# Nine dV tiles stored in three parts each, around three groups of DMA engines, in place of four tiles around one engine

## The chip, the cores and the metric

The kernel runs on one core of one Trainium2 chip. The metric is the device time of the slowest (here the only) core, in microseconds. Before the change the median of three runs was 402.31 us (402.08 to 402.5). The profiled span is some 2 us shorter than the device time of the same run (400.8 against 402.56 us), so spans are compared with spans and times with times.

## The reference

One decode step through a mix of attention and a small dense layer, and the gradients of everything. Only the attention's caches matter for the time: each is 32 heads of 4096 x 128 in bf16, 1 MB a head, read once; and their gradients have the same size and are written once.

```python
q = (x @ wq).reshape(B, Sq, H, Dh).transpose(0, 2, 1, 3)        # H = 32, Sq = 1, Dh = 128
scores = jnp.einsum("bhqd,bhkd->bhqk", q, k_cache) * (Dh ** -0.5)
p = softmax(scores, axis=-1)
o = jnp.einsum("bhqk,bhkd->bhqd", p, v_cache)
a = o.transpose(0, 2, 1, 3).reshape(B, Sq, H * Dh) @ wo
b = dense_mish(B_x, w1, b1, w2)                                 # cut
out = g * a + (1 - g) * b                                       # g = sigmoid(sum(x * gate_w))
# returned: out and the gradients of x, k_cache, v_cache, wq, wo, w1, b1, w2, gate_w
```

## The kernel before

One head after another is loaded, multiplied and stored. The loads and a few last stores are issued by SyncE (queue q1 of the profile), the gradients of K and V by GpSimd (queue q0). A tile has 128 rows (partitions) of 8 KB; a store of all 128 rows puts 8 rows on each of the 16 DMA engines.

```python
outs = ctx.enter_context(tc.tile_pool(name="outs", bufs=5))          # dK and dV tiles share it
...
def load_wo(g):
    if g < NG:
        wos[g] = wts.tile([P, G, D], BF16, name="wo_g", tag="wo_g", bufs=3)
        nc.sync.dma_start(wos[g][:], wo_v[g])                        # L136; dwo is stored from the same tile
...
def dv_half(h, half):
    st = sts[h]
    if half == 0:
        st["dV"] = outs.tile([P, J, Dh], BF16, name="dV_sb", tag="dVK")
    outer(st["dV"], st["p"], ..., half)                              # cut
    if half == 1:
        if h % 7 == 5 and h < H - 3:                                 # heads 5, 12, 19, 26
            spread(h // 7, dVv[h], st["dV"])
        else:
            ring(h).dma_start(dVv[h], st["dV"][:])

def spread(i, dst, t):
    src = t[:].rearrange("p j d -> p (j d)")
    out = dst.rearrange("p j d -> p (j d)")
    if i % 3 == 0:
        nc.gpsimd.inc_swdge_sem([], [], mode="reset_dge_cursor")
    for a, b in (((120, 125), (0, 120), (125, 128)), ((0, 14), (14, 119), (119, 128)), ((0, 8), (8, 128)))[i % 3]:
        nc.gpsimd.dma_start(out[a:b, :], src[a:b, :], max_dma_last_dim=J * Dh)
```

`spread` cuts a store into parts whose row counts decide which DMA engines take how many rows. With the cursor reset, a part of 5 rows goes to the first five engines, one row each; the part of 120 rows to the fifteen that follow, so that the fifth engine counted from the reset, "position 4", gets none; the part of 3 to positions 4, 5 and 6. Position 4 ends with 2 rows of the tile instead of 8.

## Time and profile before

| | before |
|---|---|
| time, median (range), 6 runs | 402.40 us (402.08 to 402.96) |
| span of the profiled run | 400.8 us |
| bytes over the DMA engines | 164.92 MB |
| mean rate from 12 to 375 us | 420 GB/s |
| engine time idle after 387.5 us | 3.8 us of all 16 (worked out in the prediction) |

### The profile page before, as it was taken

How to read it: one execution, taken by the hardware profiler on the slowest of the kernel's cores; microseconds unless marked ns; L12 is line 12 of the kernel's file. 1: busy time of each engine (PE TensorE's matmuls, PEld its weight loads, DVE VectorE, ACT ScalarE, POOL GpSimd, SP SyncE). 2: the span in 40 equal slices, each digit the busy share in tenths (PEclk: the TensorE clock that was granted, in tenths of full speed). 3: DMA queues.
4: the chain of work that ended last, by engine and by line, in shares of the span. 5: the costliest groups of instructions: out<-in, count | busy, mean ns of one | idle time of the engine just before them, and what ended most of it. 6: DMA issues, size and time to landing. Idle time of an engine off the chain costs nothing.

```text
span 400.8 us, 13361 instructions
## 1 busy us (share of the span) xinstructions
PE 301.0 (75%) x5752; PEld 266.0 (66%) x5752; DVE 303.1 (76%) x783; ACT 178.2 (44%) x403; POOL 47.0 (12%) x94
## 2 busy tenths in 40 slices
PE   0788888678888788768879788838888888888300
PEld 0577888567777677658868778718777678877200
DVE  3339666556799999767658999836999997898860
ACT  1455454325545555326533555604545545555000
POOL 0001111021110111211110112101111121111000
PEclk9899999959999999969977999967999999999755
DMA  8999999999999999999999999999999999999995
GB/s 292 417 407 405 418 426 421 407 423 421 424 421 424 422 422 416 422 424 424 419 424 426 422 422 417 417 425 424 421 421 424 424 423 418 425 420 418 424 383 229
DMA packets 28359, 164.92 MB, mean 412 GB/s; under 512 B 3260, under 2 KB 3964, under 8 KB 12556
## 3 DMA queue, kind: packets, MB, share of 16 engines
q1 hardware_dynamic: 17136, 93.41, 56.5%
q0 software_dynamic: 11104, 70.64, 42.3%
q8 instruction: 45, 0.74, 0.7%
q14 instruction: 14, 0.11, 0.1%
q10 hardware_dynamic: 60, 0.01, 0.0%
HBM read 82.03 MB, written 82.03 MB: 409 GB/s over the span
## 4 chain that ended last, share of the span: by engine, by line
DVE 38%; DMA 32%; PE 20%; ACT 5%; issue 3%; ACTq 0%; SPq 0%
DMA Kn<-in_A_k_cache_dram 30%; DVE dK_sb L605 9%; DVE dV_sb L605 9%; PE tr L580 8%; DVE junk L378 5%; ACT tT L582 4%; DVE junk L278 3%; PE sA L660 3%; PE sA L589 3%; PE sB L713 3%; DVE junk L530 2%; DVE wo_g L367 1%; DMA vec_rows<-in_gate_w_dram 1%; DVE dj L700 1%; DVE dwq_t L732 1%
## 5 line engine op out<-in xcount | busy, mean ns | idle before, releaser
L582 ACT COPY tT<-tr 128x512 f32<-128x512 f32 x256 | 142.4, 587 | 127.8 <-PE tr L580 126.0
L589 PEld LDWEIGHTS <-tT 128*128 128x128 bf16 x2048 | 79.8, 98 | 40.3 <-ACT tT L582 34.6
L580 PE MATMUL tr<-ident_f,Kn 128*128 128x128 f32 x512 | 81.6, 297 | 9.2 <-DMA Kn<-in_A_k_cache_dram 9.2
L605 DVE TENSOR_TENSOR dV_sb<-p_bf,qd 128x2048 bf16<-128x2048 bf16 x64 | 78.0, 1218 | 0.2 <-issue 0.2
L605 DVE TENSOR_TENSOR dK_sb<-ds_bf,qd 128x2048 bf16<-128x2048 bf16 x64 | 77.7, 1216 | 0.0
L580 PE MATMUL tr<-ident_f,Vn 128*128 128x128 f32 x512 | 72.9, 278 | 0.0
L580 PEld LDWEIGHTS tr<-ident_f,Kn 128*128 128x128 f32 x512 | 61.0, 152 | 10.4 <-issue 10.4
L589 PE MATMUL sA<-qd,tT 128*128 128x48 bf16 x1024 | 48.7, 187 | 23.8 <-ACT dq_all L718 12.7
L580 PEld LDWEIGHTS tr<-ident_f,Vn 128*128 128x128 f32 x512 | 56.3, 142 | 0.0
L589 PE MATMUL sB<-qd,tT 128*128 128x48 bf16 x1024 | 46.0, 183 | 0.0
L660 PEld LDWEIGHTS <-Vn 128*128 128x128 bf16 x1024 | 30.2, 95 | 10.9 <-issue 10.9
L660 PE MATMUL sA<-e_bf,Vn 128*128 128x48 bf16 x1024 | 30.7, 183 | 8.1 <-DVE zs L680 6.5
L622 POOL DMA_DIRECT2D out_dram<-dK_sb x30 | 17.2, 574 | 138.9 <-DVE rz L682 86.5
L713 PE MATMUL sB<-ds_bf,Kn 128*128 128x48 bf16 x1024 | 32.2, 186 | 1.4 <-DVE ds_bf L702 1.4
L664 DVE TENSOR_REDUCE m<-sA 128x1 f32<-128x32 f32 x32 | 6.1, 189 | 32.9 <-PE sA L589 26.4
L713 PEld LDWEIGHTS <-Kn 128*128 128x128 bf16 x1024 | 29.5, 98 | 1.6 <-issue 1.6
L635 POOL DMA_DIRECT2D out_dram<-dV_sb x26 | 14.1, 542 | 135.8 <-DVE o_all L705 53.4
L278 DVE SCALAR_TENSOR_TENSOR junk<-wo_g,da_bc 128x640 bf16<-128x640 bf16 x32 | 26.2, 820 | 1.7 <-ACT da_bc L229 1.1
L378 DVE SCALAR_TENSOR_TENSOR junk<-wq_g,dq_bc 128x1024 bf16<-128x1024 bf16 (+1 forms) x25 | 25.1, 1005 | 0.2
L700 DVE TENSOR_SCALAR_CACHE_REDUCE dj<-sB,rz 128x128 f32<-128x128 f32 x32 | 11.1, 346 | 13.2 <-PE sB L694 13.2
L289 PE MATMUL q_ps<-wq_g,cols_bf 128*128 128x512 bf16 x40 | 13.1, 469 | 10.5 <-DMA wq_g<-in_A_wq_dram 10.5
L684 ACT ACTIVATE p_bf<-e_bf,rz 128x64 bf16<-128x64 bf16 x32 | 11.1, 348 | 13.9 <-DVE rz L682 11.1
(148 smaller groups left out, 268.8 us busy)
## 6 DMA issues: line engine op xcount, KB each, us to landing
Kn<-in_A_k_cache_dram SPq DMA_DIRECT2D x32, 1024.0 KB, 24.0
Vn<-in_A_v_cache_dram SPq DMA_DIRECT2D x32, 1024.0 KB, 28.0
out_dram<-dK_sb POOLq DMA_DIRECT2D x30, 1024.0 KB, 11.8
out_dram<-dV_sb POOLq DMA_DIRECT2D x26, 1024.0 KB, 11.8
wq_g<-in_A_wq_dram SPq DMA_DIRECT2D x4, 1280.0 KB, 23.2
wo_g<-in_A_wo_dram SPq DMA_DIRECT2D x8, 640.0 KB, 17.6
out_dram<-wo_g POOLq DMA_DIRECT2D x7, 640.0 KB, 11.8
out_dram<-dwq_t SPq DMA_DIRECT2D x4, 896.0 KB, 17.5
```

The lines of the kernel that those rows point to most:

```text
L278: nc.vector.scalar_tensor_tensor(junk[:, 0:D], in0=wos[g][:, i, :], scalar=1.0, in1=da_bc[:], op0=ALU.mult, op1=ALU.mult, accum_out=gp["do ...
L289: nc.tensor.matmul(q_ps[:], lhsT=x_bf[:, rc:rc + 1].to_broadcast([P, P]), rhs=wq[:, rc, off:off + GD], start=(rc == 0), stop=(rc == RC - 1))
L378: nc.vector.scalar_tensor_tensor(junk[:, c0:c1], in0=wqs[w][:, rc, c0:c1], scalar=1.0, in1=dq_bc[:, w * WG * Dh + c0:w * WG * Dh + c1], op ...
L580: nc.tensor.transpose(tp[:, t, :], flat[:, k * P:(k + 1) * P], ident_f[:])
L582: nc.scalar.copy(sb[:].rearrange("p a b -> p (a b)"), tp[:].rearrange("p a b -> p (a b)"))
L589: nc.tensor.matmul(out[:, 2 * k:2 * k + W], lhsT=tb[:, t, par, :], rhs=vec[:, par, :].unsqueeze(1).to_broadcast([P, W // 2, 2]), start=(pa ...
L605: nc.vector.tensor_tensor(dst[:, a:b, :].rearrange("p j (a b) -> p j a b", b=2), col[:, a:b, :].unsqueeze(2).to_broadcast([P, n, Dh // 2, 2]),
L622: ring(h).dma_start(dKv[h], st["dK"][:])
L635: ring(h).dma_start(dVv[h], st["dV"][:])
L660: nc.tensor.matmul(O, lhsT=vts[h][:, j, :], rhs=st["e"][:, j:j + 1].to_broadcast([P, W]), start=(j == 0), stop=(j == J - 1))
L700: nc.vector.tensor_scalar(dj[:], PT, rz[:], None, ALU.mult, ALU.add, accum_out=dd[:])
L713: nc.tensor.matmul(DQ, lhsT=kts[h][:, j, :], rhs=ds[:, j, 0:1].to_broadcast([P, W]), start=(j == 0), stop=(j == J - 1))
```

## The change

Its intent: five engines run dry some microseconds before the others, so rows are to be moved away from all that end late, not from position 4 alone. Nine tiles are cut in parts: two leave out positions 9 to 14, three leave out 0 to 3, four leave out 4. "Leave out" is again 2 rows for 8. This is the whole diff:

```diff
         if half == 1:
-            if h % 7 == 5 and h < H - 3:
-                spread(h // 7, dVv[h], st["dV"])
+            if h in SPREAD:
+                spread(SPREAD[h], dVv[h], st["dV"])
             else:
                 ring(h).dma_start(dVv[h], st["dV"][:])
 
-    def spread(i, dst, t):
+    N4 = ((120, 125), (0, 120), (125, 128))
+    N6 = ((113, 128), (0, 100), (100, 113))
+    N03 = ((124, 128), (0, 108), (108, 124))
+    SPREAD = {3: N03, 6: N6, 9: N4, 12: N03, 15: N6, 18: N4, 21: N03, 24: N4, 27: N4}
+
+    def spread(parts, dst, t):
         src = t[:].rearrange("p j d -> p (j d)")
         out = dst.rearrange("p j d -> p (j d)")
-        if i % 3 == 0:
-            nc.gpsimd.inc_swdge_sem([], [], mode="reset_dge_cursor")
-        for a, b in (((120, 125), (0, 120), (125, 128)), ((0, 14), (14, 119), (119, 128)), ((0, 8), (8, 128)))[i % 3]:
+        nc.gpsimd.inc_swdge_sem([], [], mode="reset_dge_cursor")
+        for a, b in parts:
             nc.gpsimd.dma_start(out[a:b, :], src[a:b, :], max_dma_last_dim=J * Dh)
```

## The prediction

> **What bounds the kernel now.** I read the shares by engine first, then the slices of the DMA row, the queues, the chain that ended last, the windows, and last the DMA queue's own waits and issues.
>
> ```profile
> span 400.8 us, 13361 instructions
> ...
> PE 301.0 (75%) x5752; PEld 266.0 (66%) x5752; DVE 303.1 (76%) x783; ACT 178.2 (44%) x403; POOL 47.0 (12%) x94
> ...
> DMA  8999999999999999999999999999999999999995
> ...
> DMA packets 28359, 164.92 MB, mean 412 GB/s; under 512 B 3260, under 2 KB 3964, under 8 KB 12556
> ...
> q8 instruction: 45, 0.74, 0.7%
> ```
>
> No compute engine is above 76%, while the DMA row shows 9 in every slice but the first and last: 164.92 MB cross 16 DMA engines that never rest. The compute part of the chain of waits (DVE 38%, DMA 32%) only tells that DVE is next in line. The last line, instruction fetch, looks negligible; it is not, since it falls on some engines alone.
>
> ```profile
> 12.00:375.00 363.00, 296.83 (x5713) 263.39 (x5712) 287.99 (x727) 175.33 (x397) 46.05 (x82) 0.94 1.01 420
> 375.00:387.50 12.50, 1.33 (x25) 0.90 (x24) 11.03 (x38) 0.15 (x1) 0.00 (x0) 0.51 1.01 423
> 387.50:390.50 3.00, 0.28 (x1) 0.09 (x1) 0.05 (x1) 0.25 (x1) 0.00 (x0) 0.50 0.70 291
> 390.50:394.50 4.00, 0.00 (x0) 0.00 (x0) 0.00 (x0) 0.00 (x0) 0.00 (x0) 0.50 0.95 377
> 394.50:397.00 2.50, 0.00 (x0) 0.00 (x0) 0.00 (x0) 0.00 (x0) 0.00 (x0) 0.50 0.64 250
> 397.00:399.50 2.50, 0.00 (x0) 0.00 (x0) 0.00 (x0) 0.00 (x0) 0.00 (x0) 0.50 0.28 101
> ```
>
> The last two columns are the DMA share and GB/s. Up to 387.5 us all 16 engines work (1.01 counts a fetch beside a queued packet); then 0.70 is 11 of 16 (five have run dry), 0.95 once new work came, and 0.64 and 0.28 as the late engines finish one by one. Idle engine time: 3.0 x 0.30 + 4.0 x 0.05 + 2.5 x 0.36 + 2.5 x 0.72 = 3.8 us of all 16. This is all that perfect balance could win, 0.9%.
>
> ```profile
> SPq L368 <- DMA out_dram<-dV_sb: 9.8, 1, 9.8
> ...
> SPq L786 <- DMA out_dram<-dwq_t: 1.8, 1, 1.8
> ```
>
> The last two stores are held until older stores have landed on their slowest engine (issues at 389.73 and 391.90 us in the timeline), so the slowest engine sets even when the others get their last work.
>
> **Which engines are late.** The trace gives each DMA packet's start, length, size and queue, not its engine. On a busy engine a packet starts 3 or 4 ns before the one before it ends, so packets chain into 16 sequences (a search that also demands 8 rows and one 4 byte semaphore write per store held together from 36 to 334 us and again from 336 to 389 us). The 4 KB packets of the dV tiles stored in parts tell which position a sequence has: only positions 0 to 4 carry a part of 5 rows, only 4 to 6 one of 3, and 4 misses the large part. I number positions from the reset cursor. The sequences show:
> - An 8 KB row takes a slot of 306 ns (26.8 GB/s).
> - Position 4 is slow by itself: its rows last 323 ns on average against 309 to 312 elsewhere; with smaller packets, 12.1 us lost from 36 to 334 us and 2.9 us from 336 to 388 us, with no gaps.
> - The 45 fetches (16 KB, about 1 us each) go round eight sequences: positions 5 and 6, four of 7 to 12 and two of 13 to 15. Each costs a 0.95 us pause and some 0.4 us after it; 5 or 6 apiece make 6.7 to 8.1 us.
> - Two of 0 to 3 carry most of the single 8 KB loads of another queue; one of them is among the last.
> The five that run dry are two of 0 to 3 and three free of fetches among 7 to 15. Without their waits they would end near 391.0 us; position 4 and one of 0 to 3 end at 399.3, the fetchers at 396.2 to 398.9.
>
> **What the Trainium skill says.** "DMA: Bandwidth & Descriptors", section "Why a DMA increments its semaphore by 16 and not by 1": the engines of a copy number the largest k up to 16 that divides the slowest dimension; a GpSimd copy with k below 16 takes k consecutive engines from a round-robin cursor. The trace agrees: the part of 105 rows put 14 packets of 4 KB (7 rows) on each of 15 sequences and none on position 4. Section "Queues, rings and completion order": an engine alternates between queues by packet; the trace shows loads and stores alternating one for one. Section "Where 436 GB/s comes from": a fabric ceiling of 435 GB/s; the windows show 420 to 423. Section "Latency and other measured facts" calls engines 7 and 15 usually slower; here position 4 is.
>
> **The change part by part.** Bytes, compute order and waits stay; the instruction order moves no other engine. Nine stores of 128 rows are cut into three parts. Rows per engine against the plain 8:
> - leave out 4 (parts 5, 120, 3; k 5, 15, 3): 0 to 6 get +1, except 4 with -6.
> - leave out 9 to 14 (parts 15, 100, 13; k 15, 10, 13): 0 to 5 get 12 (+4), 6 to 8 and 15 get 11 (+3), 9 to 14 get 2 (-6).
> - leave out 0 to 3 (parts 4, 108, 16; k 4, 12, 16): 0 to 3 get 2 (-6), the rest 10 (+2).
>
> Sums after (4, 2 and 3 tiles): 0 to 3: 4+8-18 = -6; 4: -24+8+6 = -10; 5: 4+8+6 = +18; 6: 4+6+6 = +16; 7, 8 and 15: 6+6 = +12; 9 to 14: -12+6 = -6. Before, the four tiles (the second and third differ a little in their ends): 0 to 3 +3; 4: -25; 5, 6: +2; the others +1. So the change moves 0 to 3 by -9 rows, 4 by +15, 5 by +16, 6 by +14, 7, 8 and 15 by +11, 9 to 14 by -7.
>
> Times 0.306 us (0.32 for the slow position 4):
> - 0 to 3: -2.8 us, the latest from 399.3 to 396.5
> - 9 to 14: -2.1 us, to about 394 to 397
> - 7, 8, 15: +3.4 us, free ones to about 394.4
> - **4: +4.8 us, from 399.3 to 404.1**
> - **5 and 6: +4.9 and +4.3 us, from about 397 to 398 to about 402 to 403**
>
> The relief is right for most engines, but the two new patterns give back what the old one took from 4, and 5 and 6, which also fetch, get the largest additions. The latest end moves by about +4.8 us.
>
> GpSimd: 98 to 116 entries, 16 more issues of about 0.6 us (1.92 us for three in the timeline) and seven more cursor resets of 18 ns; at 12% busy this lies beside the rest. A semaphore write takes a 6 ns slot; 16 more stores put 0.1 us on each engine. Buffers: stores took 12 to 20 us to land; the tile's buffer is wanted again five tiles later, some 21 us after issue at about 5 us a tile, so a few more us could make DVE wait late in the run, beside the same bound.
>
> **Rivals.**
> - Balance wins. If fetches fall on other engines in this build, or if position 4's slowness goes with something else, up to 3.8 us could come back: about 399 us. For it: the aim of the change, and that five engines do run dry early. Against: position 4 gets 15 rows more whatever fetches do, and never paused.
> - It cancels. If end waits hide 2 us of the shift, 403 to 404 us. For it: the last stores wait for semaphores anyway. Against: a late engine keeps a backlog and needs no wait to be late.
> - It grows. If buffers held by stores late on 4, 5 and 6 stall DVE (9 tenths in many late slices), or loads landing late stall PE, and the late engines themselves run dry, 408 to 411 us. For it: loads already land with a spread up to 14 us between engines. Against: nothing paused there before.
>
> **Range and chances.** 402.3 + 4.8, less about half a us for the last stores' smaller packets overlapping and for rows that my count may miss: 406.6. Range 402.8 to 409.0: below lies the winning rival, above the stalls. Faster by 2% needs 8 us, over twice the idle time there is. Slower by 2% is above 410.4.
>
> **What would show it.** Right: the share falls below 16 engines earlier than 387.5 us, with a longer tail in which only about three engines work; the held store is issued at about 394 instead of 389.7; stores in parts land later than 12.9 us; HBM bytes equal. The sequence with 4's row time (323 ns) ends last, near 404. Wrong: all 16 working past 390 and a tail under 4 us (balance), or DVE waiting on stored tiles (stall).

## More of the kernel before

The prediction shows the main views. Five more lines of the kernel before are needed for comparison later: the GB/s of the 40 slices and the median time from issue to landing of a gradient's store (both from the page), and what SyncE's queue waited for at the load of a wo tile (line: microseconds in total, times, longest).

```profile
GB/s 292 417 407 405 418 426 421 407 423 421 424 421 424 422 422 416 422 424 424 419 424 426 422 422 417 417 425 424 421 421 424 424 423 418 425 420 418 424 383 229
...
out_dram<-dK_sb POOLq DMA_DIRECT2D x30, 1024.0 KB, 11.8
out_dram<-dV_sb POOLq DMA_DIRECT2D x26, 1024.0 KB, 11.8
```

```profile
SPq L136 <- DMA out_dram<-wo_g: 57.0, 5, 13.4
```

The reader is to see that the rate never leaves a narrow band between the second slice and the last two, and that there are waits for stores already (a wo tile is loaded into the buffer from which a dwo tile is stored), which cost nothing so long as other transfers fill the engines.

## The result, and the profile after

| | before | after |
|---|---|---|
| time, median (range), 6 runs each | 402.40 us (402.08 to 402.96) | 408.35 us (407.68 to 409.93) |
| ratio, 95% interval | | 1.0154 (1.013 to 1.0177) |
| profiled span | 400.8 us | 406.5 us |
| mean rate from 12 to 375 us | 420 GB/s | 416 GB/s |

Outputs are right. A ratio here is the mean time of one kernel's runs over that of the other's runs of the same rounds, so it is not quite the ratio of the quoted medians. The change made the kernel 5.95 us slower by the medians: under 2%, but far outside the scatter of either kernel.

First the page of the kernel after: the span, the rate by slice, the packets and the bytes of memory.

```profile
span 406.5 us, 13385 instructions
...
GB/s 292 418 408 404 422 423 415 421 422 422 418 423 423 419 420 415 418 428 421 421 421 423 422 414 361 406 424 403 413 378 422 424 424 421 417 419 417 414 385 166
DMA packets 29784, 164.92 MB, mean 406 GB/s; under 512 B 4045, under 2 KB 4749, under 8 KB 14621
...
HBM read 82.03 MB, written 82.03 MB: 404 GB/s over the span
...
out_dram<-dK_sb POOLq DMA_DIRECT2D x30, 1024.0 KB, 17.1
out_dram<-dV_sb POOLq DMA_DIRECT2D x21, 1024.0 KB, 16.9
```

The bytes are the same. Against the row of before there are two differences. The last slice falls from 229 to 166 GB/s: a longer, thinner tail. And in the middle there are holes that were not there: slices 25, 28 and 30, counted from 1, show 361, 403 and 378 where before had 417, 424 and 421. Stores that were not cut at all take 17 us to land instead of 12, since a transfer has landed only when its slowest engine is through.

The windows of the kernel after, with the columns of the prediction's windows (busy time by engine, granted clock, DMA share, GB/s):

```profile
12.00:375.00 363.00, 292.75 (x5603) 259.70 (x5602) 280.84 (x713) 172.74 (x390) 53.99 (x93) 0.94 1.01 416
375.00:387.50 12.50, 6.31 (x137) 5.39 (x135) 11.31 (x25) 2.94 (x8) 0.00 (x0) 0.69 1.01 418
387.50:390.50 3.00, 0.45 (x1) 0.18 (x1) 2.90 (x15) 0.00 (x0) 0.00 (x0) 0.50 1.01 419
390.50:394.50 4.00, 0.00 (x0) 0.00 (x0) 3.76 (x14) 0.00 (x0) 0.00 (x0) 0.50 0.98 403
394.50:397.00 2.50, 0.28 (x1) 0.09 (x1) 0.01 (x1) 0.26 (x1) 0.00 (x0) 0.50 0.75 304
397.00:400.00 3.00, 0.00 (x0) 0.00 (x0) 0.00 (x0) 0.00 (x0) 0.00 (x0) 0.50 0.86 322
400.00:403.00 3.00, 0.00 (x0) 0.00 (x0) 0.00 (x0) 0.00 (x0) 0.00 (x0) 0.50 0.31 117
403.00:406.40 3.40, 0.00 (x0) 0.00 (x0) 0.00 (x0) 0.00 (x0) 0.00 (x0) 0.50 0.08 28
```

From 375 to 390.5 us all engines still work, where the kernel before had 0.70 from 387.5. Then the tail. Cut finer, three single microseconds of it:

```profile
401.00:402.00 1.00, 0.00 (x0) 0.00 (x0) 0.00 (x0) 0.00 (x0) 0.00 (x0) 0.50 0.19 78
402.00:403.00 1.00, 0.00 (x0) 0.00 (x0) 0.00 (x0) 0.00 (x0) 0.00 (x0) 0.50 0.20 79
...
404.00:405.00 1.00, 0.00 (x0) 0.00 (x0) 0.00 (x0) 0.00 (x0) 0.00 (x0) 0.50 0.09 32
```

A share of 1/16 is one engine, and one engine moves about 27 GB/s: 0.19 with 78 GB/s is three engines, 0.09 with 32 is one and a bit. Three engines work for three microseconds, all others idle.

The idle sums up as in the prediction, but here to the end of the span: 4.0 x 0.02 + 2.5 x 0.25 + 3.0 x 0.14 + 3.0 x 0.69 + 3.4 x 0.92 = 6.3 us of all 16 engines. The prediction's 3.8 us stop at 399.5 us; to the end of its span the kernel before idles 3.8 + 1.3 = 5.1 us. The holes cost (420 - 416) / 420 x 363 = 3.5 us of traffic at the full rate by the rounded rates, and 4.1 us by the bytes (150.90 MB moved between 12 and 375 us, before 152.61). Together 1.2 + 4.1 = 5.3 us, against 5.7 us of span; the shares are rounded. So **on the mean engine** most of the loss lies in the middle of the run. That doesn't yet say what set the end: an engine that is early anyway may lose time in the middle for nothing.

The waits of the kernel after at the same places (SyncE's queue; then VectorE):

```profile
SPq L136 <- DMA out_dram<-wo_g: 75.4, 5, 20.2
...
SPq L368 <- DMA out_dram<-dV_sb: 8.2, 1, 8.2
```

```profile
DVE dV_sb L605 <- DMA out_dram<-dK_sb: 4.2, 2, 3.6
```

The load of a wo tile waits 18 us more in sum, and VectorE, which never waited for a store before, does so twice. The first hole shows how. SyncE's issues, first of the kernel before, then after (start, duration):

```profile
223.80 0.47 SPq L126 DMA_DIRECT2D Vn<-in_A_v_cache_dram  x1
236.97 0.33 SPq L136 DMA_DIRECT2D wo_g<-in_A_wo_dram  x1
```

```profile
225.39 0.98 SPq L126 DMA_DIRECT2D Vn<-in_A_v_cache_dram  x1
246.65 0.33 SPq L136 DMA_DIRECT2D wo_g<-in_A_wo_dram  x1
```

SyncE issues in order, so while it waits with the wo load, no K or V load goes out either: 13 us before, 21 us after. In the trace the dwo store that it waits for was issued at 227.35 us and landed on its sixteen engines between 237.47 and 246.60 us, on fifteen of them by 242.63 us and on the last one 4 us later; before, between 235.16 and 236.92. From 243 to 251 us the load queue was nearly dry (172 and 227 KB of its packets start in these two stretches of 4 us; before 711 and 758 KB), and from 243 to 256 us the rate was 364 GB/s against 415.

### The profile page after: what moved, and what is told of

It is laid out like the page before. It is cut to its first block, busy times and chain, and to the rows that moved or that the text cites. A ratio compares the mean times of both kernels' runs of the same rounds, so it can differ in the third digit from the quotient of the medians.

```text
span 406.5 us, 13385 instructions
## 1 busy us (share of the span) xinstructions
PE 302.4 (74%) x5752; PEld 267.0 (66%) x5752; DVE 302.9 (75%) x783; ACT 178.4 (44%) x403; POOL 55.0 (14%) x105
## 2 busy tenths in 40 slices
DMA packets 29784, 164.92 MB, mean 406 GB/s; under 512 B 4045, under 2 KB 4749, under 8 KB 14621
## 4 chain that ended last, share of the span: by engine, by line
DVE 35%; DMA 34%; PE 20%; ACT 5%; issue 3%; ACTq 0%; SPq 0%; DVEq 0%
DMA Kn<-in_A_k_cache_dram 27%; DVE dK_sb L605 9%; DVE dV_sb L605 8%; PE tr L580 8%; DMA out_dram<-dK_sb 6%; ACT tT L582 4%; DVE junk L378 4%; DVE junk L278 3%; PE sA L664 3%; PE sA L589 3%; PE sB L717 3%; DVE junk L487 1%; DMA vec_rows<-in_gate_w_dram 1%; DVE wo_g L367 1%; DVE dj L704 1%
## 5 line engine op out<-in xcount | busy, mean ns | idle before, releaser
L635 POOL DMA_DIRECT2D out_dram<-dV_sb x21 | 11.5, 549 | 120.0 <-DVE o_all L709 43.4
L289 PE MATMUL q_ps<-wq_g,cols_bf 128*128 128x512 bf16 x40 | 13.5, 482 | 16.3 <-DMA wq_g<-in_A_wq_dram 16.3
L647 POOL DMA_DIRECT2D out_dram<-dV_sb x27 | 17.2, 641 | 46.1 <-DVE dV_sb L605 22.8
## 6 DMA issues: line engine op xcount, KB each, us to landing
out_dram<-dK_sb POOLq DMA_DIRECT2D x30, 1024.0 KB, 17.1
out_dram<-dV_sb POOLq DMA_DIRECT2D x4, 960.0 KB, 19.2
```

The costliest lines, as they stand in the source:

```text
L289: nc.tensor.matmul(q_ps[:], lhsT=x_bf[:, rc:rc + 1].to_broadcast([P, P]), rhs=wq[:, rc, off:off + GD], start=(rc == 0), stop=(rc == RC - 1))
```

## The experiments

Every edit is to the dictionary of the kernel after, except where buffers are named. N4, N6 and N03 are its three cuts. The table gives, for all, the rows by position against 8 per plain store, worked out as in the prediction, and what came of it. "Mid-run loss" is (420 - rate) / 420 x 363 us, from the rate between 12 and 375 us; the rate is shown in whole GB/s, so this is good to about 0.9 us at worst (the kernel after has 4.1 us by its bytes).

| kernel | 0 to 3 | 4 | 5, 6 | 7, 8, 15 | 9 to 14 | median us | ratio (95%) | mid-run loss |
|---|---|---|---|---|---|---|---|---|
| before | +3 | -25 | +2 | +1 | +1 | 402.40 | 1 | 0 |
| after | -6 | -10 | +18, +16 | +12 | -6 | 408.35 | 1.0154 (1.013 to 1.0177) | 3.5 |
| e1_four_only | +4 | -24 | +4 | 0 | 0 | 402.79 | 1.0007 (0.9992 to 1.0022) | 0 |
| e4_none | 0 | 0 | 0 | 0 | 0 | 409.67 | 1.0181 (1.0166 to 1.0196) | 0.9 |
| e5_even_five | +4 | -24 | +4 | 0 | 0 | 402.61 | 1.0007 (0.9992 to 1.0021) | 0 |
| e7_leave_456 | -2 | -10 | -10, -12 | +20, +16, +16 | -2 | 407.9 | 1.0129 (1.0112 to 1.0146) | 2.6 |
| e2_n4_n6 | +12 | -16 | +12, +10 | +6 | -12 | 408.7 | 1.0157 (1.0138 to 1.0176) | 4.3 |
| e3_n4_n03 | -14 | -18 | +10 | +6 | +6 | 404.96 | 1.0062 (1.0048 to 1.0076) | 2.6 |
| e9_more_n4 | -3 | -28 | +21, +19 | +12 | -6 | 413.73 | 1.0272 (1.0253 to 1.029) | 6.9 |
| e8_six_tiles | -3, -5 | -28 | -1, -2 | +13, +11, +11 | +2 | 402.60 | 1.0003 (0.999 to 1.0017) | 0.9 |

### Which part of the change costs: e1, e4, e5

The theory was that only the layout of rows counts. The rival was that the parts themselves cost: 27 parts instead of 11 (11 more issues in all, since five whole stores fall away), seven more cursor resets and more 4 KB packets.

```diff
# e1_four_only
-    SPREAD = {3: N03, 6: N6, 9: N4, 12: N03, 15: N6, 18: N4, 21: N03, 24: N4, 27: N4}
+    SPREAD = {9: N4, 18: N4, 24: N4, 27: N4}
```

> The changed kernel with the four tiles that leave out position 4 alone (heads 9, 18, 24, 27); the two that leave out 9 to 14 and the three that leave out 0 to 3 are stored whole. Theory (the engine with the largest sum of rows and own losses sets the end): rows against 8 are -24 at position 4 (before -25), +4 at 0 to 6, so the last packet ends about 399.6 us and the time is 402.3 to 403.0. Rival (more parts, cursor resets and small packets cost the time wherever the rows go): also near 402.5, since there are as many tiles in parts as before.

Measured: 402.79 us (402.67 to 402.93), like before. Moving the four tiles from heads 5, 12, 19, 26 to 9, 18, 24, 27 and resetting the cursor at each costs nothing, so the five new tiles are what costs.

```diff
# e5_even_five
+    EVEN = ((0, 16), (16, 112), (112, 128))
-    SPREAD = {3: N03, 6: N6, 9: N4, 12: N03, 15: N6, 18: N4, 21: N03, 24: N4, 27: N4}
+    SPREAD = {3: EVEN, 6: EVEN, 9: N4, 12: EVEN, 15: EVEN, 18: N4, 21: EVEN, 24: N4, 27: N4}
```

> The changed kernel with the four tiles that leave out 4 kept, and the five others cut in three parts of 16, 96 and 16 rows, which give every engine 8 rows: same number of parts, resets and 4 KB packets as the changed kernel, no shift of rows. Theory: as with the four alone, 402.3 to 403.3. Rival (parts, resets, 4 KB packets cost the 6 us): 407.5 to 409.

Measured: 402.61 us (402.38 to 403.51). The five new tiles are cut in three here too, with resets, but each engine gets 8 rows of each. 29240 packets (after: 29784, before: 28359) and no cost: the rival falls. The store queue has 2304 packets of 4 KB in both kernels; the 544 packets that the kernel after has more are semaphore writes, 34 an engine, which at the 6 ns slot of the prediction are 0.2 us. **It is shown that where the rows go makes the difference, and neither parts, nor resets, nor 4 KB packets.**

```diff
# e4_none
+    SPREAD = {}
```

> No tile in parts at all. Theory: position 4 gets back 25 rows of 0.32 us against before, its last packet ends about 407.3 us, time 409.5 to 411, with a tail of one engine alone for about 8 us. Rival (parts cost time by themselves): faster than before, or equal, 401 to 402.5.

Measured: 409.67 us (409.58 to 410.26), as expected. Three single microseconds of its tail:

```profile
403.00:404.00 1.00, 0.00 (x0) 0.00 (x0) 0.00 (x0) 0.00 (x0) 0.00 (x0) 0.50 0.06 26
404.00:405.00 1.00, 0.00 (x0) 0.00 (x0) 0.00 (x0) 0.00 (x0) 0.00 (x0) 0.50 0.06 24
405.00:406.00 1.00, 0.00 (x0) 0.00 (x0) 0.00 (x0) 0.00 (x0) 0.00 (x0) 0.50 0.07 24
```

A share of 0.06 and some 25 GB/s: exactly one engine. Here position 4 is the only one with more rows than before (25), all others have 1 to 3 fewer, so this one engine is position 4, and the program waits for it. 25 rows at 0.323 us are 8.1 us; the time rose by 7.2 us against the kernel before on the same chip (402.43). So with the same rows on every engine one engine ends last by 4.4 us (its last packet ends at 406.39 us, the next engine's at 401.96), and this gives a price of about 0.29 us for a row on it. That it is position 4 follows from the row counts; the trace doesn't name it.

### Position 4, or positions 5 and 6: e7 and e9

The prediction named two late groups. e7 takes the new load off 5 and 6 and leaves position 4 as it is in the kernel after; e9 takes it off 4 and leaves 5 and 6.

```diff
# e7_leave_456
+    N456 = ((117, 124), (0, 117), (124, 128))
-    SPREAD = {3: N03, 6: N6, 9: N4, 12: N03, 15: N6, 18: N4, 21: N03, 24: N4, 27: N4}
+    SPREAD = {3: N03, 6: N6, 9: N456, 12: N03, 15: N6, 18: N456, 21: N03, 24: N456, 27: N456}
```

> The changed kernel with the four tiles that leave out 4 cut 7, 117, 4 instead, so that they leave out 4, 5 and 6. Rows against 8: 4 still -10, 5 -10, 6 -12, 7 +20, 8 and 15 +16, 9 to 14 -2, 0 to 3 -2. Theory with position 4 as sufficient cause: last packet still at 404 to 405 us, time 407 to 408.4, but one engine in the tail instead of three. Rival (positions 5 and 6, which also fetch instructions, set the end): 402 to 403.5.

Measured: 407.9 us (407.32 to 408.66). 28 rows fewer on each of 5 and 6 brought half a microsecond by the medians, one by the ratios. Two single microseconds of its tail:

```profile
401.00:402.00 1.00, 0.00 (x0) 0.00 (x0) 0.00 (x0) 0.00 (x0) 0.00 (x0) 0.50 0.06 25
...
403.00:404.00 1.00, 0.00 (x0) 0.00 (x0) 0.00 (x0) 0.00 (x0) 0.00 (x0) 0.50 0.06 22
```

Where the kernel after had three engines, one is left. By the sums it is position 4, with 15 rows more than before; position 7 was given 19 and can't be excluded if it is one of the fetchers, so the name of this engine is argued, its number shown.

```diff
# e9_more_n4
-    SPREAD = {3: N03, 6: N6, 9: N4, 12: N03, 15: N6, 18: N4, 21: N03, 24: N4, 27: N4}
+    SPREAD = {3: N03, 5: N4, 6: N6, 9: N4, 12: N03, 14: N4, 15: N6, 18: N4, 20: N4, 21: N03, 24: N4, 27: N4}
```

> The changed kernel with three more tiles (heads 5, 14, 20) that leave out 4. Rows against 8: 4 -28, 5 +21, 6 +19, 0 to 3 -3, the others as in the changed kernel. Theory that each of 4, 5, 6 alone is enough: 5 and 6 end at 403 to 404 us, time 406 to 407.5, two engines in the tail. Rival (position 4 alone sets the end, 5 and 6 do not): 401.5 to 402.5.

Measured: 413.73 us (412.07 to 414.28). With 18 rows less on position 4 and three more on 5 and 6 the kernel got 5.4 us slower, not faster. Its tail at 407 us and after:

```profile
407.00:408.00 1.00, 0.00 (x0) 0.00 (x0) 0.00 (x0) 0.00 (x0) 0.00 (x0) 0.50 0.11 46
408.00:409.00 1.00, 0.00 (x0) 0.00 (x0) 0.00 (x0) 0.00 (x0) 0.00 (x0) 0.50 0.13 49
```

Two engines, as 5 and 6 would be. So relieving position 4 is no cure while 5 and 6 are loaded, and the direction is the theory's; but the size is missed by some 6 us. Three rows each are about 1 us. The rest may lie in the middle of the run, where this kernel lost 6.9 us of traffic; that is not shown.

### The two new cuts one at a time: e2 and e3

```diff
# e2_n4_n6
+    SPREAD = {6: N6, 9: N4, 15: N6, 18: N4, 24: N4, 27: N4}
# e3_n4_n03
+    SPREAD = {3: N03, 9: N4, 12: N03, 18: N4, 21: N03, 24: N4, 27: N4}
```

> Four tiles that leave out 4 and the two that leave out 9 to 14; the three that leave out 0 to 3 stored whole. Rows against 8: 4 -16, 0 to 3 and 5 +12, 6 +10, 9 to 14 -12. Theory: positions 4 and one of 0 to 3 end about 402.1 us, time 404.8 to 406.0. Rival (the two patterns share the loss only through late stores and a stalled DVE, seen as DVE waiting on stored tiles): within 1 us of before unless that wait shows.

> Four tiles that leave out 4 and the three that leave out 0 to 3; the two that leave out 9 to 14 stored whole. Rows against 8: 4 -18, 5 and 6 +10, 7 to 15 +6, 0 to 3 -14. Theory: position 4 ends about 401.5 us, time 404.2 to 405.5. Rival as for the run with 9 to 14: within 1 us of before.

Measured: e2 408.7 us (407.85 to 410.13), e3 404.96 us (404.83 to 405.32). e3 is as the sums have it. e2 is 3 us over: two tiles that leave out 9 to 14 cost, on top of the four N4 tiles, all that the whole change costs. The three N03 tiles cost 2.2 us alone, and nothing on top of those two (after is no slower than e2). Each N6 tile gives six early engines' rows to ten others, position 4 and the fetching 5 and 6 among them. But 9 more rows on position 4 are 2.9 us, and e2 lost 6.1 us against before on its chip. As in e9 the surplus comes with holes in the middle of the run (4.3 us of traffic). e3 warns against a simple story, though: it lost 2.6 us of traffic in the middle and still ended where its sum said.

### What the surplus is: e10, e11, e12

The first hole began with the wo load that waits for a late dwo store. If that wait were the cause, a fourth wo buffer would take the surplus away. The memory for it comes from one transposing buffer fewer; e12 is the control, with four N4 tiles only.

```diff
# e12 on e1, e11 on the kernel after, e10 on e9
-    tsb = ctx.enter_context(tc.tile_pool(name="tsb", bufs=4))
+    tsb = ctx.enter_context(tc.tile_pool(name="tsb", bufs=3))
-            wos[g] = wts.tile([P, G, D], BF16, name="wo_g", tag="wo_g", bufs=3)
+            wos[g] = wts.tile([P, G, D], BF16, name="wo_g", tag="wo_g", bufs=4)
-    dwq_l = wts.tile([P, RC, GD], BF16, name="dwq_l", tag="wo_g", bufs=3)
+    dwq_l = wts.tile([P, RC, GD], BF16, name="dwq_l", tag="wo_g", bufs=4)
```

> Control: the four tiles that leave out 4 alone, with a fourth buffer for the wo tiles (and three instead of four for the transposed copies tT, to make room). Theory (row sums set the end; the wait of a wo load for an old wo store empties the load queue only in layouts with more late stores): 402.0 to 403.0 as with three buffers, the load's wait on the wo store much below its 59.4 us. Rival (the buffers matter by themselves): 401 or less, or over 404 if the third tT buffer was needed.

> The changed kernel with the fourth wo buffer (three for tT). Theory: the sum for position 4 stays, last packet about 404.1 us, time 406.5 to 407.5; the about 1 us that the changed kernel lies over the sum goes with the wait of the wo loads (75.4 us). Rival (that wait causes most of the 6 us): 402 to 404. Rival (it costs nothing): 408 to 409.

> Twelve tiles in parts (three more that leave out 4) with the fourth wo buffer. With three buffers it took 413.73 us where the sums for positions 5 and 6 gave 406 to 407.5. Theory: the surplus comes from wo loads held 27 us for a wo store that lands late, which keeps all later loads back and lets the load queue of every engine run dry; with the buffer 405.8 to 407.5. Rival (the parts slow the loaded engines in another way): 411 or more.

Measured: e12 402.91 us (ratio to before 1.0009, 0.9994 to 1.0024), so the buffers by themselves cost nothing. e11 408.65 us (407.94 to 409.73), ratio 1.0156 (1.014 to 1.0172), no better than the kernel after. e10 412.07 us (411.85 to 412.89), ratio 1.0243 (1.0229 to 1.0257): 1.7 us less than e9 by the medians, 1.2 us by the ratios, and far from the 405.8 to 407.5 us that the theory wanted. **The theory that the wait for the wo buffer is the cause falls.** The traces show why. The wait is gone from both, and others have come. VectorE in e11, then in e10, at the line that writes the dV and dK tiles:

```profile
DVE dV_sb L605 <- DMA out_dram<-dK_sb: 13.5, 7, 4.9
DVE dK_sb L605 <- DMA out_dram<-dV_sb: 8.4, 4, 4.0
```

```profile
DVE dK_sb L605 <- DMA out_dram<-dV_sb: 20.3, 5, 6.1
DVE dV_sb L605 <- DMA out_dram<-dK_sb: 4.4, 5, 3.0
```

And the rate by slice, first of e9, then of e10:

```profile
GB/s 295 416 408 403 421 426 413 423 423 422 416 425 423 418 412 410 420 426 420 422 417 417 426 410 371 396 420 303 406 367 421 424 422 422 417 421 410 423 317 153
```

```profile
GB/s 298 419 407 400 421 423 414 422 422 422 417 423 425 419 418 421 422 423 422 420 424 419 418 406 376 399 405 401 414 406 329 345 335 417 423 418 417 417 418 244
```

The holes of e9 in slices 28 and 30 (303, 367) are filled, and others stand in slices 31 to 33 (329, 345, 335). This fits a backlog on the loaded engines that stays, so that the next buffer that is short takes the wait over. The natural next step, more than five dK and dV buffers, is not possible: a sixth does not fit in the on-chip memory (the build stops, some 4.7 KB per partition short).

But neither the waits nor the missing traffic measure the loss. e10 lost 9.5 us of traffic between 12 and 375 us (409 GB/s) against 6.9 in e9 and was faster; e11 lost 5.2 us (414 GB/s) against 3.5 in the kernel after, at the same time. And two kernels of the next section wait as much and are as fast as the kernel before. SyncE's queue in e8, then VectorE in e13:

```profile
SPq L136 <- DMA out_dram<-wo_g: 74.6, 5, 22.2
```

```profile
DVE dV_sb L605 <- DMA out_dram<-dK_sb: 6.4, 3, 3.6
DVE dK_sb L605 <- DMA out_dram<-dV_sb: 2.3, 1, 2.3
```

### A version that would beat both: e8, e13

If sums over positions are the key, a layout that takes from 4, 5, 6 and 0 to 3 at once should win part of the idle 3.8 us.

```diff
# e8_six_tiles (e13_six_wo4: the same with the buffers of e12)
+    N456 = ((117, 124), (0, 117), (124, 128))
+    N04 = ((121, 126), (0, 121), (126, 128))
+    SPREAD = {3: N04, 8: N456, 13: N6, 17: N04, 21: N456, 26: N4}
```

> A new layout worked out from the sums: six tiles in parts (5, 121, 2 twice; 7, 117, 4 twice; 15, 100, 13 once; 5, 120, 3 once). Rows against 8: 4 -28, 5 -1, 6 -2, 0 and 1 -3, 2 and 3 -5, 7 +13, 8 and 15 +11, 9 to 14 +2. Theory: no engine ends after 398.5 us, time 401.0 to 402.0, that is 0.4 to 1.4 us under before. Rival (more parts cost by themselves, or the sums miss something): 402.4 or more.

> The layout of six tiles worked out from the sums, with the fourth wo buffer. With three it took 402.60 us where the sums gave 401.0 to 402.0. Theory: the held loads cost it the missing us, 400.8 to 402.0 now. Rival (the sums are too hopeful by themselves): 402.4 or more.

Measured in five rounds each: e8 402.60 us (402.35 to 402.98), e13 402.57 us (402.44 to 403.12), ratios 1.0003 (0.999 to 1.0017) and 1.0005 (0.9992 to 1.0017). Both miss: they equal the kernel before and beat nothing. Nothing tried here is faster than the kernel before.

## Why the prediction was right or wrong

The time, 408.35 us, lies in the range and near its upper end; the centre was 1.75 us too low. By its own steps:

- **Bound: DMA engines.** Right. Bytes unchanged, no compute engine busier, and e4 and e1 move the time by 7 us with nothing but the place of rows changed.
- **At most 3.8 us to win.** Not contradicted; "balance wins" didn't happen, here or in e8.
- **The late ends move by +4.8 us; position 4 last, 5 and 6 just before.** The direction is right, and most of the size. The held store was issued at 395.44 us ("about 394"), three engines are busy from 401 to 404 us, the last is through at 405.07 us (predicted 404.1), the large parts of the cut stores take 13.7 to 19.2 us to land (predicted over 12.9). The sums give e4, e1, e3 and e5 within their expectation, and e4 shows position 4 alone in the tail. That 5 and 6 are also late enough is supported by e9, whose tail has two engines. That all three names in the tail of the kernel after are right, and that position 4 is the last of them, is argued from the sums and not shown.
- **"The share falls below 16 engines earlier than 387.5 us".** Wrong. It stayed at 1.01 to 390.5 us and at 0.98 to 394.5 us, and "all 16 working past 390" is half of what the prediction had named as a sign of being wrong (the other half, a tail under 4 us, didn't come). The engines that were relieved of rows did not run dry sooner, because 1.7 MB that the kernel before had moved by 375 us were still to be moved: the sums had no term for time lost in the middle of the run.
- **Cost of parts, resets and small packets near nothing.** Right, shown by e5, though the counts were off: 11 more issues and not 16, since five whole stores fall away, and 49 more semaphore writes an engine, which at 6 ns are 0.3 us and not 0.1.
- **Waits on buffers: "a few more us could make DVE wait late in the run, beside the same bound".** This is the weakest step. It got no term of its own, and about half a microsecond was even taken off the sum for other reasons. The runs showed VectorE waiting 4.2 us for stored dK tiles, PE waiting 16.3 us for wq loads (10.5 before), the wo load 18 us longer, and 3.5 us of traffic missing between 12 and 375 us. Not late in the run, either: the holes lie at 244 to 305 us. VectorE waiting on stored tiles was the other sign of being wrong that the prediction named, and the signs of the rival that was called "it grows" thus came in part. Set beside the sum of +4.8 us, the measured +5.95 us leave about 1.2 us (at e4's 0.29 us a row the sum is 4.3 us, and 1.6 us are left); in e2 and e9 the surplus over the expectation was some 3 and 6 us. That these waits carry the surplus is not shown: e8 and e13 wait as long and lose nothing, and e1 has 14.5 us of PE waits for wq.
- **"Nothing paused there before"**, the argument against that rival, was true and of no use. It describes a state with the backlog spread evenly; after the change VectorE did pause for stores.

What stays open: which wait, if any single one, carries the surplus (removing one of them moved it to the next); and how the hole reaches the late engines themselves, which have work queued. In the first hole the engines were not idle (the DMA share from 243 to 256 us was 1.00, at 364 GB/s): some packets lasted longer. The stores' 8 KB packets that start there took 351 ns on the mean (before: 313), yet three quarters of them took at most 314 ns, and the longest 1180. This would slow a late engine without letting it go idle, if the long packets are on it. Followed as the prediction follows them, the packets of the sequence with the slow rows don't show it: it moved 98 to 103 KB in each 4 us of the hole, and 98 to 106 KB around it. Such sequences are not certain, and no run here isolates this. e3, with 2.6 us of missing traffic and no surplus, and e10, with more of it than e9 and less time, show that missing traffic alone doesn't decide.

## What to carry to other kernels

When the DMA engines bound a kernel, what counts is the sum of work on each engine, with each engine's own speed and its extra duties. Before rows are moved to "the others", find out which of the others are late themselves: here each of the two new cuts relieved early or middling engines and paid with the slow one. And a store lands when its slowest engine is through, so skew shows twice, in the tail and in every buffer that is held longer; a sum over engines gives the first, and it takes a trace to see the second. A wait in a trace is not yet a cost: the same waits stood in kernels that lost nothing.

## What the Trainium skill lacked or had wrong

- "DMA: Bandwidth & Descriptors", section "Latency and other measured facts", calls engines 7 and 15 usually slower. Here one engine, the fifth from the cursor's reset, is slow by itself: 323 ns per 8 KB row against 309 to 312 on the others; with no row moved away from it, it alone works at the end (409.67 us against 402.43). The traces don't name hardware engines, so whether it is a number that the page means is not known.
- "Runtime: NRT & Kernel Launch", section "Instruction fetch mechanics", has the fetches as DMA transfers of 16 KiB blocks and calls their cost mostly hidden. No page that I read tells that they cost the DMA engines unevenly. In these traces, by the prediction's sequences, 45 fetches of 16 KB go round eight of the sixteen engines, a pause of 0.95 us and some 0.4 us after it each, up to 8.1 us on an engine, though the page of the profile gives them 0.7%.
- The same DMA page, section "Why a DMA increments its semaphore by 16 and not by 1", gives the rule by which a copy's rows choose engines, and the runs agree with it. It also says that only the full count of 16 means that all has landed. It lacks what follows for other transfers: uneven parts of nine stores made even uncut stores land in 17.1 us instead of 11.8 us (12.4 us with the even parts of e5).
- No page that I read tells why single packets last so much longer while few loads are queued: from 243 to 256 us of the kernel after, the stores' 8 KB packets took 351 ns on the mean and up to 1180 ns, most of them 309 ns (before: 313 ns on the mean).
